# Attention and gated unit on one core: AV of the pair before and the scores of a pair side by side at the opening of a period, reciprocals ahead of the first transposes

## The chip, the core and the metric

The kernel runs on one core of a Trainium2 chip. The core has five engines that run side by side, each through its own list of instructions in order: TensorE (PE in the profile; its weight loads stand apart as PEld), VectorE (DVE), ScalarE (ACT), GpSimd (POOL) and SyncE (SP, which here only issues DMAs). TensorE writes its results into PSUM, a small memory of eight banks per partition, from which VectorE or ScalarE must take them before a bank can be used again. The metric is the device time of one execution in microseconds (us), lower is better. Time before: median 1212.31 us of three runs (1208.61 to 1212.54).

## The reference

Eight batches of eight heads of attention over 576 positions with head size 64 and a mask by blocks of 64, then a gated unit with weights 512 x 1536 twice and 1536 x 512:

```python
scores = (1 / sqrt(64)) * q @ k.T                      # 8 x 8 heads, 576 x 576
scores = where(block_i >= block_j, scores, -1e9)       # blocks of 64 positions
attn = exp(scores - max(scores)); attn /= sum(attn) + 1e-9
x = (attn @ v) -> (4608, 512)
out = (sigmoid(x @ w_gate) * (x @ w_val)) @ w_out
```

## The kernel before, in words

**Stages.** The attention and the first third of the gated unit (`F1` = 4 of 12 column blocks of the weights) run interleaved in a first stage, about 600 us. The other eight column blocks follow in a second stage, in which TensorE multiplies by a Strassen scheme (line 834). Between them lies a handover, in which VectorE prepares weights and sums for the second stage (`early_work`, lines 758 to 769, `sums_gv`, `x_sums`).

**Pairs and periods.** Two heads make a pair, four pairs a batch: 32 pairs. The loop at line 771 has a period for each pair `p`, and one more for the last AV. `attend(p)` gives the steps of a pair:

- "s", the scores (`s_blocks`, line 378): three double PSUM banks, for the query blocks 3, 2 and (1, 0). The two heads use 64 rows of the array each (`tile_position=(64 * h, 0)`, tiles of 64x128 in the profile). Then, for each group, a mask on VectorE (line 392 or 394), the negative maximum (line 372, VectorE) and two exponentials (line 375, ScalarE) into `P3`, `P2`, `P1`, `P0`, with the row sums in `sm`.
- "t", the tail of 64 queries for both heads (`s_tail`, line 398), with its maximum (408) and exponential (410).
- "r", the reciprocals (`recip`, line 413): three small VectorE instructions on `sm`, the last of which writes `rT`, then four DMAs to `r_d` in HBM and three back into `rb`, spread over the partitions; all seven are issued by SP.
- "tr3", "tr2", "trl", "trt": transposes on TensorE (line 250) of the exponentials, each into a double bank, copied by ScalarE into `G1` and `G0` (line 350, `copy_out`), of which there is one each.
- "AV" (line 472): `G1`, `G0` times `VS` (the values), the two heads in 64 columns of the array each (tiles of 128x64), 28 matmul instructions; VectorE multiplies the result by `rb` into `xT` (line 486). `finish` (491) casts `xT` to `XH` on ScalarE, stores it to HBM as `xT_d`, and GpSimd makes the low half `XL`.
- "k" and "q": steps of `prep(p + 1)`: VectorE transposes the next pair's k and q (279), ScalarE makes their high halves (314, 315), VectorE the low halves (318, 319); the loads of pair `p + 3` are issued by SP.

AV in period `p` belongs to pair `p - 1`; all other steps of the list `REST` belong to pair `p`. Double banks come from `ps_a`, of which there are three; the gated unit's products use two single banks of their own (`ps_m`).

**Order.** The order of the steps is written out in three lists: `FIRST` for pairs 0 to 6, `TURN` for pair 7, `REST` from pair 8 on (line 32). The number beside a step is its places: after the step, that many times, some instructions of the gated unit (`mlp1`: `hidden`, line 126, and `out_mm`, line 135) are dealt, `rate` of them each (lines 795 to 809). A period has `TICKS` = 12 places. `rate` is set anew when AV of a batch's last pair has been issued (lines 780 to 784), so that by the same point four periods later all but `KEEP` = 32 instructions are dealt. On TensorE the scores and AV stand behind the matmul dealt last (lines 386, 482), transposes and dealt matmuls stand behind the last scores or AV (`hold`), and a dealt matmul may be taken up to `AHEAD` = 3 places early; within that a scheduler sets each engine's order when the program is built.

**Handover.** In the last pair's period and behind it, `early_work` loads the first weights (`raw`, into tiles that held k and q of pairs 30 and 31) and the first activations (`XB` from `xT_d`), issued by SP in order, and lets VectorE make their sums.

Of the kernel before, what the change touches and what calls it, by code (L numbers as in the profile page):

```python
# [28 lines left out]

FIRST = (("s3", 1), ("TR2", 1), ("k", 1), ("s2", 1), ("TRt", 1), ("q", 1), ("t", 1), ("TRl", 1), ("sl", 1), ("AV", 2),  # L30
         ("tr3", 1), ("r", 0), ("ld", 0))
REST = (("s", 3), ("t", 1), ("AV", 2), ("tr3", 1), ("r", 0), ("k", 0), ("tr2", 1), ("q", 0), ("trl", 2), ("trt", 2))
TURN = (("s3", 1), ("TR2", 1), ("k", 0), ("s2", 1), ("TRt", 1), ("q", 0), ("t", 1), ("TRl", 1), ("sl", 1), ("AV", 1),
        ("tr3", 1), ("r", 0), ("tr2", 1), ("trl", 1), ("trt", 1))
N_FIRST = 7
# [5 lines left out]
def attn_glu_kernel(ctx: ExitStack, tc: tile.TileContext, q, k, v, w_gate, w_val, w_out, out):  # L41
# [119 lines left out]
    with ExitStack() as s2:  # L161
# [609 lines left out]
        for p in range(n + 1):  # L771
# [3 lines left out]
            tick = 0  # L775
            for what, places in (FIRST if p < N_FIRST else TURN if p == N_FIRST else REST):
                if what.startswith(("AV", "TR")):
# [247 lines left out]
```

## Time and profile before

| | |
|---|---|
| median of three runs | 1212.31 us (1208.61 to 1212.54) |
| the profiled execution's own time | 1211.92 us |
| its span, first to last instruction | 1210.1 us |
| TensorE busy | 1167.7 us (96%), 7421 matmuls |
| VectorE busy | 770.4 us (64%) |
| ScalarE busy | 627.7 us (52%) |
| GpSimd busy | 332.6 us (27%) |
| periods of the pairs from 8 on | about 16.8 us, up to 22 us where the dealt matmuls are the longer ones of line 135 |

A row of the timeline has the start, the duration, the engine, the line of the kernel, the operation, what is written from what, and the shape; equal neighbours are merged (x28), and in brackets stands how long the engine had been idle and who released it. Durations of matmuls overlap, since they are pipelined: what an instruction costs in a stream is the distance between starts. A row of busy time by stretches has the stretch, its length, then for PE, PEld, DVE, ACT and POOL the busy time and the number of instructions, then the granted clock of TensorE, the DMA share and GB/s. A row of waits has who waited, for whom, the sum in us, how many times, and the longest. The chain of waits is the work that ended last, in order of time.

### The profile page before, as it was taken

What the parts mean: (1) busy time and instruction counts of PE and PEld (TensorE: products, weight loads), DVE (VectorE), ACT (ScalarE), POOL (GpSimd) and SP (SyncE); (2) the same over time, 40 slices, a digit from 0 to 9 for tenths busy, and PEclk for the clock granted to TensorE, in tenths of its full rate; (3) what the DMA queues carried; (4) which work ended last, traced back from release to release, by engine and by line L of the source; (5) the groups of instructions that cost most, each with busy time, mean ns of one, the idle gap of its engine ahead of it and who ended that gap; (6) DMA issues with size and microseconds to landing.
All of it is one profiled execution on the core that took longest, in us unless ns stands there. A gap on an engine that the chain in (4) does not pass through costs nothing.

```text
span 1210.1 us, 20754 instructions
## 1 busy us (share of the span) xinstructions
PE 1167.7 (96%) x7421; PEld 1025.6 (85%) x7421; DVE 770.4 (64%) x1447; ACT 627.7 (52%) x1459; POOL 332.6 (27%) x411
## 2 busy tenths in 40 slices
PE   6989899999999999999999999999999999999996
PEld 3557789888888988888789889999999999998895
DVE  5678945356454545544899976866866655755743
ACT  6776857576676666666444453453454432422420
POOL 0123223133231331322101223123122153262331
PEclk8999999999999999999999999999999999999998
DMA  8664343543544443444243335235287154164153
GB/s 179 168 150 98 97 114 74 118 87 78 118 88 105 99 102 83 98 111 120 91 129 115 106 135 200 72 129 200 59 300 288 59 179 165 55 198 155 55 157 105
DMA packets 249112, 152.52 MB, mean 126 GB/s; under 512 B 189489, under 2 KB 209969, under 8 KB 248369
## 3 DMA queue, kind: packets, MB, share of 16 engines
q1 hardware_dynamic: 237952, 132.02, 39.5%
q10 hardware_dynamic: 11056, 19.17, 4.5%
q8 instruction: 58, 0.95, 0.3%
q14 instruction: 46, 0.37, 0.1%
HBM read 103.81 MB, written 47.33 MB: 125 GB/s over the span
## 4 chain that ended last, share of the span: by engine, by line
PE 73%; DVE 12%; DMA 6%; ACT 3%; POOL 2%; issue 2%; SPq 1%; POOLq 0%; DVEq 0%; ACTq 0%
PE b L834 19%; PE m L126 13%; PE bank L247 13%; PE m L892 9%; PE m L135 6%; PE bank L250 5%; PE b L892 5%; DMA pr<-part_d 3%; DVE XL L724 2%; POOL pr L907 1%; ACT P L375 1%; DMA XB<-xT_d 1%; DVE nm L372 1%; PE m L250 1%; PE bank L126 1%
## 5 line engine op out<-in xcount | busy, mean ns | idle before, releaser
L834 PE MATMUL b<-XH,w 128*128 128x384 f32 x1344 | 352.3, 337 | 5.0 <-DVE v L870 2.5
L834 PEld LDWEIGHTS b<-XH,w 128*128 128x128 f32 x1344 | 244.9, 188 | 12.4 <-DVE v L870 5.3
L834 PE MATMUL b<-XL,w 128*128 128x384 f32 x672 | 225.2, 336 | 0.0
L375 ACT ACTIVATE P<-bank,nm 128x512 f32<-128x512 f32 (+3 forms) x256 | 133.5, 538 | 69.7 <-DVE nm L372 59.0
L834 PEld LDWEIGHTS b<-XL,w 128*128 128x128 f32 x672 | 126.6, 188 | 1.3
L892 PE MATMUL m<-wo,hH 128*128 128x512 f32 x384 | 124.9, 391 | 0.0
L372 DVE TENSOR_REDUCE nm<-bank 128x2 f32<-128x1024 f32 (+3 forms) x128 | 105.0, 820 | 29.4 <-ACT P L375 26.8
L350 ACT COPY G<-bank 128x768 f32<-128x768 f32 (+3 forms) x140 | 93.2, 696 | 29.6 <-PE bank L250 26.2
L126 PE MATMUL m<-XH,wv 128*128 128x288 f32 x448 | 104.2, 304 | 1.7 <-DVE h L147 1.7
L126 PE MATMUL m<-XH,wg 128*128 128x288 f32 x448 | 104.2, 303 | 0.0
L247 PE MATMUL bank<-G,VS 128*64 128x320 f32 (+4 forms) x896 | 98.2, 361 | 0.0
L153 POOL TENSOR_TENSOR hL<-h,hH 128x288 fp32r<-128x288 f32 (+1 forms) x56 | 42.4, 757 | 199.6 <-ACT hH L152 190.7
L907 POOL TENSOR_TENSOR pr<-pr,pr 128x512 f32<-128x512 f32 x36 | 48.0, 1333 | 162.1 <-DMA pr<-part_d 139.5
L247 PEld LDWEIGHTS bank<-G,VS 128*64 128x64 f32 x896 | 55.9, 137 | 36.9 <-issue 3.5
L723 ACT CAST XH<-XB 128x1536 fp32r<-128x1536 f32 (+2 forms) x72 | 66.1, 938 | 34.6 <-DVE XB L721 25.1
L892 PEld LDWEIGHTS m<-wo,hH 128*128 128x128 f32 x384 | 71.9, 188 | 13.7
L857 ACT ACTIVATE g<-g 128x384 f32<-128x384 f32 x72 | 37.4, 524 | 81.6 <-DVE g L870 61.1
L724 DVE TENSOR_TENSOR XL<-XB,XH 128x1536 fp32r<-128x1536 f32 (+2 forms) x72 | 77.8, 1089 | 0.9 <-ACT XH L723 0.4
L126 PEld LDWEIGHTS m<-XH,wv 128*128 128x128 f32 x448 | 74.7, 188 | 4.0 <-DVE h L147 1.9
L392 DVE MEMSET bank<- 64x128 f32 x64 | 10.6, 165 | 105.8 <-PE bank L247 105.2
L126 PEld LDWEIGHTS m<-XH,wg 128*128 128x128 f32 x448 | 74.9, 188 | 3.2 <-issue 1.8
L250 PE MATMUL bank<-ident,P 128*128 128x128 f32 x560 | 75.4, 273 | 0.8 <-DVE rT L419 0.7
(179 smaller groups left out, 2488.4 us busy)
## 6 DMA issues: line engine op xcount, KB each, us to landing
pr<-part_d SPq DMA_DIRECT2D x72, 256.0 KB
xT_d<-xT ACTq DMA_DIRECT2D x32, 288.0 KB
XB<-xT_d SPq DMA_DIRECT2D x16, 576.0 KB
part_d<-ost SPq DMA_DIRECT2D x36, 256.0 KB
out_dram<-ost SPq DMA_DIRECT2D x36, 256.0 KB
VS<-in_v_dram SPq DMA_DIRECT2D x64, 128.0 KB
part_d<-ost ACTq DMA_DIRECT2D x32, 256.0 KB
rqk<-in_k_dram SPq DMA_DIRECT2D x108, 72.0 KB
```

The lines of the kernel that those rows point to most:

```text
L126: mm = nc.tensor.matmul(ps, lhsT=lh, rhs=rh, start=(i == 0), stop=(i == n - 1))
L135: mm = nc.tensor.matmul(ps, lhsT=lh[:, f, t * P:(t + 1) * P], rhs=rh, start=(i == 0), stop=(i == n - 1))
L247: pe_last[:] = [nc.tensor.matmul(*args, **kw).ins]
L250: pe_last[:] = [nc.tensor.transpose(*args).ins]
L350: mark("ACT", nc.scalar.copy(out=dst, in_=src))
L372: mark("DVE", nc.vector.tensor_reduce(out=nm[:, c0:c0 + 2], in_=ps[:, :, c:c + n], axis=AX.X, op=ALU.max, negate=True))
L375: mark("ACT", nc.scalar.activation(out=Pi[:, h], in_=ps[:, h, c:c + n], func=AF.Exp, bias=nm[:, c0 + h:c0 + h + 1], accum_out=sm[:, 5 * h ...
L723: nc.scalar.copy(out=XO[j][0][:, a:b], in_=x)
L724: sub = nc.vector.tensor_sub(out=XO[j][1][:, a:b], in0=x, in1=XO[j][0][:, a:b].bitcast(F32))
L834: mm = nc.tensor.matmul(ps, lhsT=lh, rhs=rh, start=(first and k == 0), stop=(k == n - 1), skip_group_check=not first)
L892: mm = nc.tensor.matmul(po[t], lhsT=lh[:, f, t * P:(t + 1) * P], rhs=rh, start=(half == 0 and i == 0), stop=(half == 1 and i == 5))
L907: nc.gpsimd.tensor_add(out=pr[0], in0=pr[0], in1=pr[1])
```

## The change

One list is changed. In `REST`, AV (of pair `p - 1`) moves from behind the tail to the head of the period, with no place behind it, so that the scores of pair `p` follow it on TensorE without dealt matmuls between them. Its two places go to the scores (4 instead of 3) and to "trt" (3 instead of 2). "r" moves from behind "tr3" to ahead of it. The sum of places stays 12.

```diff
-REST = (("s", 3), ("t", 1), ("AV", 2), ("tr3", 1), ("r", 0), ("k", 0), ("tr2", 1), ("q", 0), ("trl", 2), ("trt", 2))
+REST = (("AV", 0), ("s", 4), ("t", 1), ("r", 0), ("tr3", 1), ("k", 0), ("tr2", 1), ("q", 0), ("trl", 2), ("trt", 3))
```

## The prediction

> **What bounds the kernel now.** I read the page first, then the waits of TensorE over the pairs that the change touches (195 to 600 us), then busy time by stretches, single instructions around one period, and the chain of waits.
>
> ```profile
> span 1210.1 us, 20754 instructions
> PE 1167.7 (96%) x7421; PEld 1025.6 (85%) x7421; DVE 770.4 (64%) x1447; ACT 627.7 (52%) x1459; POOL 332.6 (27%) x411
> PE 73%; DVE 12%; DMA 6%; ACT 3%; POOL 2%; issue 2%; SPq 1%; POOLq 0%; DVEq 0%; ACTq 0%
> ```
> ```profile
> PE m L126 <- DVE h L147: 1.7, 1, 1.7
> PE bank L250 <- DVE rT L419: 0.7, 1, 0.7
> ```
> ```profile
> 255.30:272.10 16.80, 16.80 (x144) 15.11 (x143) 9.57 (x20) 11.67 (x32) 5.35 (x9) 1.00 0.43 91
> ```
>
> TensorE bounds it. In 405 us it waits for another engine twice, 2.4 us in all, both at the very end (below). A whole period is busy (16.80 of 16.80) at granted clock 1.00, VectorE at 9.57, ScalarE at 11.67. So nothing can be gained here by feeding TensorE sooner: only by making its own stream shorter. What is short of peak in that stream shows at the edges of the tiled blocks, where starts lie further apart than inside (one period, opening at 401.70):
>
> ```profile
> 401.47 0.29 PE L126 MATMUL m<-XL,wv 128*128 128x288 f32 x1
> 401.70 0.50 PE L247 MATMUL bank<-KH,QH 64*128 64x512 f32 x2
> 402.03 0.41 PE L247 MATMUL bank<-KH,QL 64*128 64x512 f32 x2
> 402.27 0.41 PE L247 MATMUL bank<-KL,QH 64*128 64x512 f32 x2
> ...
> 403.71 0.53 PE L126 MATMUL m<-XH,wv 128*128 128x288 f32 x2
> 404.08 0.29 PE L126 MATMUL m<-XL,wv 128*128 128x288 f32 x1
> ...
> 407.17 0.29 PE L126 MATMUL m<-XH,wv 128*128 128x288 f32 x1
> 407.40 2.93 PE L247 MATMUL bank<-G,VS 128*64 128x320 f32 x28
> 410.25 0.40 PE L126 MATMUL m<-XL,wv 128*128 128x288 f32 x1
> 410.50 0.42 PE L126 MATMUL m<-XH,wv 128*128 128x288 f32 x2
> ...
> 418.48 0.49 PE L247 MATMUL bank<-KH,QH 64*128 64x512 f32 x2
> ```
>
> The gated-unit matmuls (L126) follow each other by 0.133 us at full stream (two take 0.42 where one takes 0.29; the second decimal is rounded). Into the scores: 401.47 to 401.70 is 0.23, 0.10 too long, and the first step inside is 0.33 where the next is 0.24, 0.09 too long: 0.19 for entering. Out of them: two steps of L126 take 0.37 (403.71 to 404.08) instead of 0.27, 0.10, and I take the 0.10 before it to be as at the entry: 0.20. Into AV: 0.23 instead of 0.13, 0.10 (a little more inside it is the same after the change). Out of AV: 0.25 instead of 0.13, 0.12, with its 0.10 before: about 0.20. A period enters and leaves two tiled blocks, four edges.
>
> **The change, part by part.** (1) AV at 0 places and the scores behind it. AV's exit (0.20) and the scores' entry (0.19) go; one edge between a block of 128x64 and one of 64x128 comes. The trace has no such edge. Below: it costs nothing, and the period gains 0.39; above: it costs like the two that went, and the gain is nil; I see no way to a loss in the stream itself. I take 0.20, since the edges seen from both sides cost 0.19 to 0.22, whichever form they lead to: 0.19 gained. Pairs 8 to 31 are 24 periods: 24 x 0.19 = 4.6 us (0 to 9.4).
>
> [...]
>
> (2) What AV's earlier place demands. Before, scores, four places and the tail stood between the last transposes of a pair and its AV; now three places of about five L126 matmuls do (15 x 0.133 = 2.0 us).
>
> ```profile
> 404.36 0.69 ACT L375 ACTIVATE P<-bank,nm 128x512 f32<-128x512 f32 x1 [2.80 <-DVE nm L372]
> 409.64 0.25 ACT L375 ACTIVATION_READ_ACCUMULATOR P<-bank,nm 128x1 f32 x1
> 411.31 0.68 ACT L314 CAST KH<-KQ 128x576 fp32r<-128x576 f32 x1 [1.41 <-DVE KQ L279]
> 417.25 0.75 ACT L350 COPY G<-bank 128x512 f32<-128x512 f32 x2 [0.87 <-PE bank L250]
> ```
> ```profile
> 411.86 0.78 DVE L486 TENSOR_TENSOR xT<-bank,rb 128x320 f32<-128x320 f32 x2
> ```
> ```profile
> 410.63 1.38 SPq L422 DMA_DIRECT2D r_d<-rT  x4
> 413.77 1.74 SPq L425 DMA_DIRECT2D rb<-r_d  x3
> ```
>
> Write S for the start of the scores. The period is 16.78 (401.70 to 418.48) and AV takes 2.85 (407.40 to 410.25), so the next AV is due at S+13.9. Its last input is the copy of the tail's transposes, 0.75 us for two, which waits for TensorE, not for ScalarE (0.87 idle before it): 2.0 us cover 0.75 and 1.2 are left. Cost nothing while ScalarE keeps up (a rival, below).
>
> (3) AV's bank is wanted again by the scores' third group (three double banks turn). VectorE frees it with two products, 0.78 us, about 0.1 after AV; the first two groups stand between: 0.33 and twice 0.24 for the first, three times an estimated 0.18 for the second, three quarters as wide, 1.3 us together. Covered by 0.4.
>
> (4) The fourth product operand, rb. Its DMAs are issued until 415.51, S+13.8. It takes 1.8 us from the end of the first four issues (412.01) to the release of the next three (413.77), a round trip; the same again puts rb at about S+15.6. It was used a period later; now at S+16.9. Covered by 1.3. The reciprocals' new place ahead of tr3 moves three small VectorE instructions and these seven issues past nothing that runs earlier: they wait for the last exponential, which ends at 409.89 (S+8.2) in either order, and on SP they stand behind nothing new. I cost it at nothing; if rb slips behind the loads of q on SP, the product waits on VectorE with the mask and the maxima of the next softmax queued behind it, and TensorE waits at the third group.
>
> (5) Transposes. tr3 now stands after scores (2.0), 20 matmuls (2.7), the tail (0.8) and 5 more (0.7): S+6.2; its exponentials, 0.69 each from S+2.66, are done. tr2 comes at S+7.8, and wants the bank of the third scores group, which ScalarE leaves at S+8.2: 0.4 short. The schedule may put matmuls of the next three ticks ahead (AHEAD), so I take nothing, at most 0.4 in those periods that deal L126 matmuls alone at 5 or so a tick (three in each of five batches, 15 of 24): 6 us.
>
> (6) The dealing. Same twelve places, but the new batch opens four places earlier, so by pair 31's scores 36 instead of 32 ticks of 5.0 have passed since pair 28's AV: 20 matmuls (2.7 us) more are done; before the last AV it is 4 of L126 and 16 of L135 more (0.133 and 0.23 each, 4.2 us). That work leaves the stage behind.
>
> **Where the gain meets the handover.** The chain of waits through the last pair, then VectorE's rows, then stretches behind it:
>
> ```profile
> 564.92 2.04 PE bank L247 x20
> 568.45 7.42 DMA XB<-xT_d
> 577.70 0.68 DVE xT L486 x2
> 582.69 0.46 DVE h L147
> ```
> ```profile
> 589.22 0.39 PE L135 MATMUL m<-wo,hH 128*128 128x512 f32 x1
> 589.44 0.39 PE L135 MATMUL m<-wo,hL 128*128 128x512 f32 x1
> ```
> ```profile
> 575.96 0.56 DVE L710 TENSOR_TENSOR XB<-XB 128x384 f32<-128x384 f32 x1 [4.25 <-DMA XB<-xT_d]
> 585.21 0.29 DVE L672 TENSOR_TENSOR cT<-cT 128x128 f32<-128x128 f32 x1
> 588.69 0.82 DVE L486 TENSOR_TENSOR xT<-bank,rb 128x320 f32<-128x320 f32 x2 [3.19 <-PE bank L247]
> ```
> ```profile
> 604.00:608.00 4.00, 4.00 (x31) 3.96 (x30) 4.00 (x10) 1.34 (x3) 0.00 (x0) 1.00 0.20 68
> 608.00:612.00 4.00, 4.00 (x32) 4.00 (x31) 4.00 (x14) 1.61 (x5) 0.00 (x0) 1.00 0.44 142
> ```
>
> Here the chain is not TensorE's. Pair 31's scores free a tile, SP goes on, XB lands 7.4 us later, VectorE has stood 4.25 us for it, works, stands 3.19 us for the last AV, and from 588.69 it is full (4.00 of 4.00). So the handover ends as early as VectorE's two idle stretches allow. Pair 31's scores move by +2.85 (AV now before them) +2.7 (more matmuls before) -23 x 0.19 = -4.4: 1.2 us later. XB with them: 577.2. VectorE's work from there to the end of the row at 585.21 was 9.5 us; 0.7 of it (the product of pair 30) is now done earlier: ready at 586.0. The last AV releases the product at 588.69; minus 4.6, plus 4.2 of work dealt before it, minus the 2.4 of waits if both vanish, gives 585.9 at best, when VectorE is not yet free. If the h product is queued behind the weight sums as it is now (582.69), the L135 matmuls dealt ahead of AV wait for it, and AV about keeps its place (eight L126 matmuls and AV's 2.85 follow that product now, some seven of L135 would then): 588.3 as an estimate. So the product comes at 586.0 to 588.3: 0.4 to 2.7 us are carried to the end, I take 1.6. The other 3.0 turn into idle time of TensorE in front of a full VectorE.
>
> **Sum.** The profiled execution took 1211.92 us (span 1210.1), 0.39 under the median 1212.31 of the three. 1211.92 - 1.6 = 1210.3; against the median 1210.7. Likeliest case's own range: 1209.6 to 1211.9. A measurement of this kernel tells about 0.3%, 3.6 us, from no change.
>
> **The rivals.** A: the handover carries it all. For it: the two TensorE waits stem from VectorE standing for XB, and the pair-30 product that stands in their way moves forward. Against: rows above, XB's landing hangs on scores that move later. 1212.3 - 4.6 = 1207.7, with the 2.4 of waits 1205.3.
>
> B: slower. ScalarE becomes the bound of a period: during AV and scores, 4.9 us on end, it gets no new work but one cast, and then has the softmax and all copies before the next AV. First exponential at S+2.66; 11.67 busy less 0.68 for the cast is 11.0: done at S+13.65 if it never waits, AV due at S+13.9. If the 1.41 us it waits for KQ stays unfilled, AV is 1.1 late, in 15 periods of L126 alone 17 us: 1212.3 - 1.6 + 17 = 1228. It decides from 0.35 us a period (5.3 us less 1.6 is 3.7). Against: tr3's copy can fill that wait, and the gated unit's share of the 11.0 falls partly outside. [...]
>
> C: no net gain, as tr2's 0.4 us (part 5) eats it: -4.6 + 6, and with the handover about 1212.3 to 1214. Or the schedule puts scores ahead of AV or splits them, so that four edges stay: 1212.
>
> **How the numbers follow.** Likeliest 0.45, A 0.25, C 0.10, B 0.20. Faster by over 0.3% is A: 0.25; same is the likeliest and C: 0.55; slower is B: 0.20. The range goes from A's lower part, 1205.5, to 1218, which takes in B up to 0.6 us a period.
>
> **What would show it.** Right: between pairs 8 and 31 a period without L135 work is 16.6 instead of 16.78; AV to scores shows a first start 0.2 after AV's last; no TensorE wait before AV; pair 31's scores near 566; VectorE still full from about 587. Wrong: TensorE waits named after ScalarE's G or P at AV or tr2, each period (B, C); VectorE starting its full stretch by 584 (A).

## The result and the profile after

The changed kernel takes 1224.84 us (median of 6 runs, 1222.60 to 1226.56) against 1210.17 us (6 runs, 1207.52 to 1212.54) of the kernel before on the same chip: ratio 1.012, 95% interval 1.0101 to 1.0138. It is slower by 14.7 us, where 1210.7 with a range up to 1218 was forecast.

The page after (span, TensorE's busy time, shares of the chain that ended last):

```profile
span 1222.8 us, 20667 instructions
PE 1173.9 (96%) x7421; PEld 1027.3 (84%) x7421; DVE 780.1 (64%) x1447; ACT 624.4 (51%) x1459; POOL 322.5 (26%) x411
PE 73%; DVE 11%; DMA 6%; ACT 3%; issue 3%; POOL 2%; SPq 1%; POOLq 0%; DVEq 0%; ACTq 0%
```

The page alone hides the loss: TensorE still has 96% and 73% of the chain. Its busy time has grown by 6.2 us for the same 7421 matmuls, so part of the loss lies inside the stream. The waits of TensorE from 125 to 600 us:

```profile
PE bank L247 <- DVE xT L486: 4.1, 4, 2.8
PE bank L247 <- ACT G L350: 1.6, 1, 1.6
PE bank L247 <- ACT P L375: 0.7, 1, 0.7
PE bank L247 <- issue: 0.2, 1, 0.2
```

6.6 us, and 4.4 of them in one place, pair 8's opening. (The kernel before waits in that period too, 2.2 us for P and G, so the waits explain little by themselves.) Three places show where the rest is.

**A usual opening (pair 22).** TensorE after:

```profile
410.50 1.84 PE L247 MATMUL bank<-G,VS 128*64 128x320 f32 x12
412.27 0.50 PE L247 MATMUL bank<-KH,QH 64*128 64x512 f32 x2
...
413.16 1.31 PE L247 MATMUL bank<-G,VS 128*64 128x64 f32 x16
414.40 0.44 PE L247 MATMUL bank<-KH,QH 64*128 64x384 f32 x2
...
415.63 0.39 PE L247 MATMUL bank<-KH,QH 64*128 64x256 f32 x2 [0.44 <-DVE xT L486]
...
416.41 0.40 PE L126 MATMUL m<-XL,wv 128*128 128x288 f32 x1
```

AV isn't one block. The first group of scores stands between its first 12 and its last 16 instructions, so the two blocks meet at three edges inside instead of one, and AV ends later. The instruction order has this in 13 of the 24 openings (pairs 8, 14 to 18, 22 to 26, 30 and 31). VectorE's rows there show what follows:

```profile
413.53 1.22 DVE L372 TENSOR_REDUCE nm<-bank 128x2 f32<-128x1024 f32 x1
414.68 0.81 DVE L486 TENSOR_TENSOR xT<-bank,rb 128x320 f32<-128x320 f32 x2
```

The maxima of the first scores now stand ahead of the product that empties AV's bank; the product ends at 415.49, and the third group, which wants that bank, starts at 415.63. The same wait of 0.44 us stands at the openings of pairs 14 and 30. And ScalarE's row for the input at which AV is cut, the second tail copy:

```profile
410.51 0.28 ACT L350 COPY G<-bank 128x128 f32<-128x128 f32 x1
```

It ends at 410.79, 1.5 us before TensorE reaches the cut at 412.27. On the chip nothing had to be waited for; the cut stands in the instruction order.

**The first opening (pair 8)** on TensorE, then SP's, VectorE's rows, then stretches:

```profile
137.89 1.84 PE L247 MATMUL bank<-G,VS 128*64 128x320 f32 x12 [1.64 <-ACT G L350]
...
145.33 0.39 PE L247 MATMUL bank<-KH,QH 64*128 64x256 f32 x2 [2.75 <-DVE xT L486]
```
```profile
135.82 1.38 SPq L422 DMA_DIRECT2D r_d<-rT  x4
139.55 1.75 SPq L425 DMA_DIRECT2D rb<-r_d  x3
```
```profile
143.78 0.67 DVE L111 SCALAR_TENSOR_TENSOR XB<-csq,XB 128x512 f32<-128x512 f32 x1
144.38 0.81 DVE L486 TENSOR_TENSOR xT<-bank,rb 128x320 f32<-128x320 f32 x2
```
```profile
142.00:146.00 4.00, 1.25 (x16) 0.94 (x14) 3.97 (x9) 2.01 (x5) 0.00 (x0) 1.00 0.42 108
146.00:149.50 3.50, 3.50 (x18) 3.40 (x15) 3.44 (x5) 2.10 (x6) 1.41 (x1) 0.51 0.25 91
```

AV of pair 7 stands at once behind pair 7's last transposes, since `TURN` ends in one place where `REST` now ends in three. TensorE waits 1.64 us for their copies. rb is still on its way (its issues end at 141.30; the transfer lands at 143.66), VectorE takes one conversion more (143.78) before the product, and TensorE stands 2.75 us for the bank. Behind that the granted clock is 0.51 for 3.4 us, which costs an estimated 1.7 (half of 3.4).

**The second stage** has one long wait that the kernel before had not. SP, GpSimd, ScalarE, VectorE and TensorE in turn, each one step later, then the stretches:

```profile
721.20 3.81 SPq L906 DMA_DIRECT2D pr<-part_d  x2
725.06 1.93 SPq L902 DMA_DIRECT2D part_d<-ost  x2
```
```profile
723.37 1.29 POOL L907 TENSOR_TENSOR pr<-pr,pr 128x512 f32<-128x512 f32 x1 [11.45 <-DMA pr<-part_d]
724.62 1.01 POOL L842 TENSOR_TENSOR hL<-t,hH 128x384 fp32r<-128x384 f32 x1
```
```profile
725.66 0.49 ACT L857 ACTIVATE t<-b 128x384 f32<-128x384 f32 x1 [3.27 <-POOL hL L842]
730.53 1.55 ACT L723 CAST XH<-XB 128x768 fp32r<-128x768 f32 x2
```
```profile
731.38 1.83 DVE L724 TENSOR_TENSOR XL<-XB,XH 128x768 fp32r<-128x768 f32 x2 [2.16 <-ACT XH L723]
733.12 0.55 DVE L870 TENSOR_TENSOR v<-b,v 128x384 f32<-128x384 f32 x1
```
```profile
733.73 0.69 PE L834 MATMUL b<-XH,w 128*128 128x384 f32 x1 [3.09 <-DVE v L870]
```
```profile
729.00:733.00 4.00, 1.64 (x10) 1.32 (x8) 1.84 (x3) 4.00 (x8) 0.00 (x0) 1.00 0.43 131
733.00:736.50 3.50, 2.77 (x8) 2.68 (x9) 3.50 (x8) 2.77 (x3) 0.00 (x0) 0.52 0.00 0
```

GpSimd waits 11.45 us for a load of pr that the second half of this stage needs (SP holds it in line between two stores of ost); hL behind it, t on ScalarE, the casts XH, XL on VectorE and v all come late, TensorE stands 3.09 us, and the clock is halved once more (0.52 from 733.0 to 736.5 us).

### The profile page after: what moved, and what is told of

Same layout as the page of the kernel before. It is cut to its first block, busy times and chain, and to the rows that moved or that the text cites. A ratio compares the mean times of both kernels' runs of the same rounds, so it can differ in the third digit from the quotient of the medians.

```text
span 1222.8 us, 20667 instructions
## 1 busy us (share of the span) xinstructions
PE 1173.9 (96%) x7421; PEld 1027.3 (84%) x7421; DVE 780.1 (64%) x1447; ACT 624.4 (51%) x1459; POOL 322.5 (26%) x411
## 4 chain that ended last, share of the span: by engine, by line
PE 73%; DVE 11%; DMA 6%; ACT 3%; issue 3%; POOL 2%; SPq 1%; POOLq 0%; DVEq 0%; ACTq 0%
PE b L834 20%; PE m L126 13%; PE bank L247 13%; PE m L892 9%; PE m L135 6%; PE bank L250 5%; PE b L892 5%; DMA pr<-part_d 2%; DVE XL L724 2%; ACT P L375 1%; PE m L250 1%; POOL pr L907 1%; DMA out_dram<-ost 1%; DMA rb<-r_d 1%; DVE ost L908 1%
## 5 line engine op out<-in xcount | busy, mean ns | idle before, releaser
L834 PE MATMUL b<-XH,w 128*128 128x384 f32 x1344 | 352.4, 337 | 9.3 <-DVE v L870 3.7
L834 PEld LDWEIGHTS b<-XH,w 128*128 128x128 f32 x1344 | 245.0, 189 | 16.4 <-DVE v L870 6.7
L834 PE MATMUL b<-XL,w 128*128 128x384 f32 x672 | 225.5, 336 | 0.0
L834 PEld LDWEIGHTS b<-XL,w 128*128 128x128 f32 x672 | 126.7, 189 | 1.2
L126 PE MATMUL m<-XH,wv 128*128 128x288 f32 x448 | 104.5, 305 | 0.0
L126 PE MATMUL m<-XH,wg 128*128 128x288 f32 x448 | 104.1, 303 | 0.0
L486 DVE TENSOR_TENSOR xT<-bank,rb 128x320 f32<-128x320 f32 x64 | 26.3, 452 | 120.0 <-PE bank L247 95.9
L247 PE MATMUL bank<-G,VS 128*64 128x320 f32 (+4 forms) x896 | 101.1, 363 | 1.6 <-ACT G L350 1.6
L496 POOL TENSOR_TENSOR XL<-xT,XH 128x576 fp32r<-128x576 f32 x32 | 46.4, 1451 | 182.6 <-ACT XH L493 171.4
L126 PEld LDWEIGHTS m<-XH,wv 128*128 128x128 f32 x448 | 76.0, 190 | 1.4 <-issue 0.5
L126 PEld LDWEIGHTS m<-XH,wg 128*128 128x128 f32 x448 | 75.5, 189 | 1.9 <-issue 0.9
L892 PE MATMUL m<-wo,hL 128*128 128x512 f32 x192 | 75.6, 394 | 0.0
```

The costliest lines, as they stand in the source:

```text
L126: mm = nc.tensor.matmul(ps, lhsT=lh, rhs=rh, start=(i == 0), stop=(i == n - 1))
L247: pe_last[:] = [nc.tensor.matmul(*args, **kw).ins]
L834: mm = nc.tensor.matmul(ps, lhsT=lh, rhs=rh, start=(first and k == 0), stop=(k == n - 1), skip_group_check=not first)
L892: mm = nc.tensor.matmul(po[t], lhsT=lh[:, f, t * P:(t + 1) * P], rhs=rh, start=(half == 0 and i == 0), stop=(half == 1 and i == 5))
```

## The experiments

Each ratio is to runs of the kernel before on the same chip: 1208.35 us beside experiments 1 to 4, 1209.33 beside 5 to 7, 1208.84 beside 8 to 10 and 1208.71 beside 11 and 12. Added lines shift the numbers in their rows by up to four. Where the trace is read at fixed points, these are the start of pair 9's scores, of pair 31's scores, of the first product of the second stage (L834 in the kernel before) and of TensorE's last matmul. In the kernel before they are at 157.8, 564.8, 641.5 and 1199.7 us, after at 168.0, 578.5, 650.0 and 1212.3. Kernels 5 and 12 have the same first stage, and their first products lie 2.8 us apart (641.8 and 639.0), so differences of 1 or 2 us at that point say little by themselves. A trace is one execution: those of 5, 8 and 10 took 5.1, 2.4 and 3.0 us more than the median of their runs, so sums of costs below go by the medians.

**1. Scores behind the whole AV, in all pairs.**

```diff
+                        if av_last and k == j == 0:
+                            behind(first_mm[0], av_last[0])
...
+                av_last[:] = pe_last
```

> The changed kernel with one order added: the scores of a pair stand behind the last matmul of AV on TensorE, so that AV cannot be split. Theory (the split is the scheduler's choice; on the chip the copies that AV needs were done long before): all 24 openings become one AV and one scores block; the 13 split ones lose 0.56 to 1.04 us each (the first, of pair 8, keeps its wait for rb), 9.8 us in all: 1214 to 1217 us. Rival (ScalarE is really late for AV): TensorE then waits inside AV for the G copies, 0.5 us or more in some ten periods, and the time stays at 1221 or above.

1224.92 us, ratio 1.0139 (1.0122 to 1.0155). All 24 openings are whole, and from pair 9's scores to pair 31's it is 404.1 us instead of 410.5 after and 407.0 before. But the hold also acted on pairs 0 to 7, whose lists were not meant: pair 9's scores start at 176.6 instead of 168.0. So this total, above the 1214 to 1217 expected, tells nothing about the splits; experiment 5 repeats it from pair 8 on alone.

**2. The list of before in the period of pair 8 alone.**

```diff
+REST8 = (("s", 3), ("t", 1), ("AV", 2), ("tr3", 1), ("r", 0), ("k", 0), ("tr2", 1), ("q", 0), ("trl", 2), ("trt", 2))
...
-            for what, places in (FIRST if p < N_FIRST else TURN if p == N_FIRST else REST):
+            for what, places in (FIRST if p < N_FIRST else TURN if p == N_FIRST else REST8 if p == N_FIRST + 1 else REST):
```

> The changed kernel with the old list in the period of pair 8 alone, the new list from pair 9. Theory: the 1.6 us for a G copy, the 2.8 us for the product that waits for rb, and the slower TensorE clock behind them (13 matmuls at 0.24 instead of 0.13 us, 1.4 us) go, about 6 us; splits stay in about ten of the 23 remaining openings (in others than before): 1215 to 1219 us. Rival (the waits of pair 8 are absorbed later anyway): 1222 to 1226.

1211.49 us, ratio 1.003 (1.002 to 1.0041). One period out of 24 gives back 11.6 of the 14.7 us, more than expected, although ten openings are still split.

**3. Both edits, 1 and 2.**

> Both: scores held behind AV, and the old list for pair 8. Theory (nothing else costs): 23 openings save 0.19 us each, 4.4 us, of which the handover lets 0.4 to 4.4 us through: 1206 to 1210, or 0.2 to 4.4 us below the kernel before. Rival (the new place of AV costs something on its own, as tr2 waiting for its bank): above the kernel before by 2 us or more, with TensorE waits in each period.

1215.29 us, ratio 1.006 (1.0044 to 1.0076). Missed, for the reason of experiment 1: pair 9's scores start at 171.2 although pair 8 has its old list.

**4. "r" back behind "tr3".** Otherwise as changed.

```diff
-REST = (("AV", 0), ("s", 4), ("t", 1), ("r", 0), ("tr3", 1), ("k", 0), ("tr2", 1), ("q", 0), ("trl", 2), ("trt", 3))
+REST = (("AV", 0), ("s", 4), ("t", 1), ("tr3", 1), ("r", 0), ("k", 0), ("tr2", 1), ("q", 0), ("trl", 2), ("trt", 3))
```

> The changed kernel with the reciprocals back behind the first transposes. Theory (they wait for the last exponential in either place, so their place in the list decides nothing): the same as the changed kernel, 1222 to 1227. Rival (their earlier place helps or hurts by 2 us or more through SP's queue): a difference of over 3 us.

1226.79 us, ratio 1.015 (1.0131 to 1.0169): the intervals of this and of the change overlap. The order on every engine is the same in both, instruction by instruction. The move of the reciprocals is worth nothing, as forecast. (Its second stage takes 564.5 us by the trace, the change's 562.3: so much can lie between two executions of one order.)

**5. Scores behind the whole AV, from pair 8 on** (edit 1 with `if rest and av_last and ...`).

> The changed kernel, with the scores held behind the last matmul of AV on TensorE only from pair 8 on (the earlier hold also acted on pairs 0 to 7, where it cost time of its own). So all 24 openings are unsplit and pairs 0 to 7 are as in the changed kernel. Theory (two causes: splits in 13 openings, and the opening of pair 8, where TensorE waits for the copies to G and for rb): pair 9's scores still start near 168.0 us, since in pair 8 the wait for rb ends at the same instant whether AV is split or not; from there to pair 31's scores 404.1 us instead of 410.5, as in the earlier hold; of these 6.4 us nearly all reach the end, because VectorE's handover hangs on pair 31's scores and the last AV: 1216 to 1219, still slower than before. Rival 1 (the splits are the whole loss): 1209 or less. Rival 2 (the handover takes what the splits give back, the splits cost nothing): 1223 to 1226, with the first product of the second stage near 650 as in the changed kernel.

1212.73 us, ratio 1.0031 (1.0013 to 1.0048). Pair 9's scores start at 168.0 and pair 31's 403.6 later, both as the theory had them, but the total falls by some 11 us instead of 6 to 9. The same opening of pair 22, TensorE and VectorE:

```profile
406.93 2.93 PE L247 MATMUL bank<-G,VS 128*64 128x320 f32 x28
409.79 0.50 PE L247 MATMUL bank<-KH,QH 64*128 64x512 f32 x2
...
410.95 0.34 PE L247 MATMUL bank<-KL,QH 64*128 64x384 f32 x2
411.23 0.39 PE L247 MATMUL bank<-KH,QH 64*128 64x256 f32 x2
...
412.00 0.40 PE L126 MATMUL m<-XL,wv 128*128 128x288 f32 x1
```
```profile
410.25 0.82 DVE L489 TENSOR_TENSOR xT<-bank,rb 128x320 f32<-128x320 f32 x2 [3.34 <-DMA rb<-r_d]
```

The two blocks take 5.07 us (406.93 to 412.00) instead of 5.91 (410.50 to 416.41): a split costs 0.84 here, and thirteen at that price would be an estimated 10.9 us, about what the total fell by. The product still waits for rb, but only 0.1 us of it reaches TensorE (411.23 for 411.13).

**6. Edits 5 and 2 together.**

> Both remedies: the list of before for the period of pair 8 alone, and scores behind the whole AV from pair 8 on, with pairs 0 to 7 left as they are. Theory: pair 9's scores near 158.8 us (as with the old list for pair 8), then 406.3 us to pair 31's scores and 474 us to the first product of the second stage (as with the earlier hold and the old list, which had both remedies but a disturbed start), then the second stage as before: 1203 to 1208, faster than before by 0.2 to 0.6%. Rival (a cost of the new order beyond splits and pair 8, about 3 us by the first run with both remedies): 1209 to 1213. Rival (the handover takes it back): first product of the second stage near 641 as with the old list for pair 8 alone, 1210 to 1212.

1210.14 us, ratio 1.0009 (0.9999 to 1.002): missed, no gain. The trace splits it in two. The first product of the second stage comes at 637.1, 4.4 us earlier than before; from there to the last matmul it takes 562.6 us instead of 558.2, so all of it is lost again in the second stage, where TensorE waits 3.5 us for v and the clock is halved behind that, as shown above for the change (matmuls of 128x384 start 0.32 us apart at 721.5, 0.18 apart at 730.2).

**7. The new list for pair 8 alone**, the list of before from pair 9 on.

> The new list in the period of pair 8 alone, the list of before from pair 9 on: one split opening instead of 13, so the price of pair 8's opening by itself. Theory: pair 9's scores about 7.3 us later than before (10.2 in the changed kernel, less 2.86 for an AV that stands ahead of them there), 165.1 us; the rest keeps its lengths, so 1216 to 1219 without further loss, and up to 1221 if the later loss in the second stage (two stretches of half clock there instead of one) belongs to pair 8's delay. Rival (pair 8's opening is harmless by itself and the loss comes from the order of later pairs): 1209 to 1213.

1212.98 us, ratio 1.0034 (1.0022 to 1.0047). TensorE stands 1.66 us for G and 2.76 for the product as in the change, and pair 9's scores start at 163.8, near the 165.1 expected. By itself this opening costs 3.6 us: the waits at pair 8 are 2.2 us longer than before (4.4 for 2.2), and a stretch of half clock behind them (from 145.4 to 148.5 us matmuls of 128x288 start 0.24 us apart, at 149.0 0.13) costs an estimated 1.7. The total lies where the rival expected it, but above before by more than the interval.

**8 to 10. pr's loads held back in the second stage**: on both remedies (8), on the kernel before (9), on the change (10).

```diff
-                        nc.sync.dma_start(out=part2_d[r:r + P, :], in_=ost)
+                        stored[:] = [nc.sync.dma_start(out=part2_d[r:r + P, :], in_=ost).ins]
...
-                        mark2("SP", nc.sync.dma_start(out=tile_, in_=src[r:r + P, :]))
+                        d = nc.sync.dma_start(out=tile_, in_=src[r:r + P, :])
+                        behind(d.ins, stored[0])
+                        mark2("SP", d)
```

> Both remedies as in the run before (list of before in pair 8's period alone, scores behind the whole AV from pair 8 on), and in the second stage the loads of pr (L906) held on SP behind the last store of the first round of blocks, so that they no longer stand between the stores of ost. In both remedies alone the first product of the second stage came 4.4 us earlier than before (637.1 against 641.5), and the second stage gave 4.3 us back: from its first product to TensorE's last 562.5 us against 558.2, with one wait of 3.5 us for VectorE at 717 to 721 and a stretch of half clock behind it. Theory (the scheduler's other order in the second stage costs this, by the loads of pr on SP and what stands behind them): the wait goes, second stage 556 to 559 us, total 1203 to 1206, faster than before by 0.3 to 0.5%. Rival (the second stage is bound by VectorE's work from the handover on, so that an earlier start only turns into waits): first product near 637, second stage still 562, total 1209 to 1211.

> Control: the kernel before with the same hold on the loads of pr alone. Its second stage has no such wait (2.0 us for VectorE's g once), so theory: within 1 us of before, 1208 to 1210, second stage 557 to 559. If it is faster than before by as much as the kernel with both remedies is, the gain there is the hold's and not the new order's.

> The changed kernel with the same hold on the loads of pr alone. Its second stage took 562.3 us against 558.2 of before, with a wait of 3.1 us for VectorE's v and half clock from 733. Theory (three causes: pair 8's opening, the splits, the second stage's order): the first product of the second stage stays near 650, the second stage falls to 557 to 559, total 1219 to 1222. Rival (the second stage's loss follows from a late handover, whatever its order): total 1223 to 1226.

8: 1207.28 us, ratio 0.9985 (0.9973 to 0.9997). 9: 1208.44, ratio 0.9999 (0.9988 to 1.001). 10: 1219.95, ratio 1.0088 (1.0072 to 1.0104). The hold is worth nothing on the kernel before and 3.6 us on the change (14.7 to 11.1). 9 and 10 came as expected; 8 lies between the 1203 to 1206 of its theory and the 1209 to 1211 of its rival. In 8, TensorE's wait shrinks but stays:

```profile
PE b L838 <- DVE g L874: 2.6, 1, 2.6
PE b L838 <- DVE v L874: 2.4, 3, 1.8
```

The longest wait for v is 1.8 instead of 3.5, the stage 560.0 us instead of 562.6. So the order of pr's loads is one part. The rival, that a full VectorE turns an earlier start into waits, is not shown for the rest: VectorE is as full in kernel 11 (below) as in 6, whose first products come at 636.3 and 637.1, and the second stage of 11 takes 557.1 us. Kernel 6, then 11:

```profile
640.00:665.00 25.00, 23.92 (x137) 23.39 (x137) 25.00 (x49) 11.38 (x21) 4.76 (x4) 1.00 0.25 80
```
```profile
640.00:665.00 25.00, 23.93 (x136) 23.14 (x135) 25.00 (x49) 11.27 (x20) 4.75 (x4) 1.00 0.20 60
```

**11 and 12. What AV of pair 7 lacks.** 12 is the change with edit 5 and the hold on pr; 11 is that with three of pair 8's places moved ahead of AV ("ld" does nothing in this period).

```diff
+REST8 = (("ld", 3), ("AV", 0), ("s", 3), ("t", 1), ("r", 0), ("tr3", 1), ("k", 0), ("tr2", 1), ("q", 0), ("trl", 1), ("trt", 2))
```

> The changed kernel with scores behind the whole AV from pair 8 on and the loads of pr held back in the second stage, the new list from pair 8 on: what is left of the loss is pair 8's opening alone. Theory: pair 9's scores near 168.0 us with the waits of 1.6 us for G and about 2.8 us for the product (rb) at pair 8 and a stretch of half clock behind them; total as the kernel with both remedies and the same hold (1207.3) plus the 2.6 us that pair 8 cost between the two kernels that have the unsplit order (1212.7 against 1210.1): 1209 to 1212.

> The same kernel, with three of pair 8's twelve places moved ahead of AV of pair 7 (one each from the scores, trl and trt), so that some ten matmuls more stand on TensorE between pair 7's last transposes and that AV. Theory (AV of pair 7 comes too early for the copies to G and for rb, since pair 7's own list leaves one place or none behind its last transposes): the wait for G of 1.6 us goes, the wait for the product shrinks from 2.8 to about 1.5 us, too short for the stretch of half clock; pair 9's scores fall from 168.0 to 162.5 to 164 us; the total falls by 1 to 3 us against the kernel without it, to 1207 to 1210. Rival (the loss at pair 8 lies in the scores' and transposes' order there, not in AV's inputs): pair 9's scores stay at 167 or later and the total does not fall.

12: 1209.17 us, ratio 1.0006 (0.9989 to 1.0023). 11: 1206.26, ratio 0.9984 (0.9972 to 0.9997). In the trace of 11 at pair 8:

```profile
138.46 2.93 PE L248 MATMUL bank<-G,VS 128*64 128x320 f32 x28 [1.66 <-ACT G L351]
...
144.79 0.38 PE L248 MATMUL bank<-KH,QH 64*128 64x256 f32 x2 [1.97 <-DVE xT L490]
```

The numbers came in, the mechanism mostly not. The wait for G stays (the dealt matmuls spread between the transposes, which moved with AV), and the wait for the product falls to 1.97, from 2.60 in 12, with the half clock behind it all the same (0.50 from 145.9 to 149.3 us). That 1.5 us would be too short for it was the author's estimate; behind the changed kernel's wait of 1.64 us the clock is 1.00 (138 to 142 us). Pair 9's scores start at 163.6 instead of 167.2, but ten matmuls of L135 fewer lie ahead of them, some 2.3 us that are merely done later. 11 is faster than 12 by 2.9 us; in the traces its first product of the second stage comes 2.7 us earlier (636.3 for 639.0), and that stage takes 557.1 us instead of 558.7, in an order on TensorE and VectorE that no other kernel here has. So the gain is not shown to be AV's later place.

## Why the prediction was wrong, point by point

The start of AV's last product on VectorE, then the starts of TensorE, us, and the totals against before. "Order" names the second stage's order of instructions on TensorE and VectorE, which is the same in every kernel with the same letter:

| kernel | list at pair 8 | AV | AV's last product | first product, 2nd stage | from it to the last matmul | order | total, us |
|---|---|---|---|---|---|---|---|
| before | old | apart | 588.7 | 641.5 | 558.2 | a | 0 |
| 9 (before, pr held) | old | apart | 587.6 | 640.2 | 558.7 | a | -0.4 |
| 7 | new | split at 8, then apart | 591.0 | 645.1 | 556.6 | a | +3.6 |
| 6 | old | whole | 588.9 | 637.1 | 562.6 | b | +0.8 |
| 5 | new | whole | 592.9 | 641.8 | 563.0 | b | +3.4 |
| changed | new | split | 600.6 | 650.0 | 562.3 | b | +14.7 |
| 8 (6 with pr held) | old | whole | 589.1 | 637.2 | 560.0 | b | -1.6 |
| 12 (5 with pr held) | new | whole | 590.1 | 639.0 | 558.7 | b | +0.5 |
| 10 (changed, pr held) | new | split | 602.1 | 651.5 | 558.8 | b | +11.1 |
| 2 | old | split | 593.0 | 641.1 | 558.2 | its own | +3.1 |
| 11 | new, AV later | whole | 588.3 | 636.3 | 557.1 | its own | -2.4 |

**The step that failed** is a premise of part 1 and of the likeliest case, taken without a reason: that the schedule would keep AV whole and that 24 periods are alike, pair 8's included. Rival C named the split, but as no dearer than the four edges of before. What the runs showed in its place, by the totals: the splits cost 11.3 us (5 to the change), the new list at pair 8 costs 2.6 (6 to 5), and with neither the kernel is 0.8 slower than before: 14.7 together. With the loads of pr held it is 10.6 (12 to 10), 2.0 (8 to 12) and -1.6.

Kernel 6 is the nearest to what was predicted, with 23 new openings instead of 24. Its first product of the second stage comes 4.4 us earlier, where part 1 had 4.6, but that is luck: AV's last product, through which the forecast carried the gain, starts 0.2 us later than before. The 4.4 come from the handover behind it, 48.2 us instead of 52.8; it takes 48.0 to 49.5 in the table's kernels of order b or of an order of their own, and 52.7 to 54.1 in those of order a. Nothing in the prediction had that.

The second stage was not in the prediction either. In order b (kernels 1 and 4 have it too) it takes 562.3 to 564.5 us, whether it starts at 637 or at 650, and 558.7 to 560.0 with the loads of pr held; in order a 556.6 to 558.7, held or not. So these 4 us belong to the order, with pr's loads as the main part of it, and not to a late or an early start.

(1) The edge was about right. Pair 21's scores before, then in kernel 5:

```profile
384.94 0.50 PE L247 MATMUL bank<-KH,QH 64*128 64x512 f32 x2
```
```profile
393.24 0.51 PE L247 MATMUL bank<-KH,QH 64*128 64x512 f32 x2
```

Pair 22's follow at 401.70 and 409.79: the period takes 16.55 us against 16.76, with 60 dealt matmuls in both, 0.21 gained for 0.19 forecast. Not every period gains it. The next one takes 17.00 in kernel 5 and 16.75 in kernel 12, against 16.78 before; in both kernels, dealt matmuls stand between the last of its transposes. Over the 22 periods from pair 9's scores to pair 31's, kernels 5 and 12 are 3.4 and 3.7 us shorter than before (403.6 and 403.4 for 407.0), about 0.16 a period; their 20 dealt matmuls of L126 more and 12 of L135 fewer cancel.

(2) AV's last input was in time on the chip in the usual openings, as worked out, and this did not help: the instruction order is fixed when the program is built, and there AV is cut at the piece that takes the second tail copy. That the scheduler reckons this copy later than the chip has it is argued from where the cut stands, not shown. What the hold shows is that nothing on the chip forced it: with AV whole, behind pair 8 TensorE waits for the copies at AV 0.19 and 0.16 us in kernel 5 and not at all in 12.

(3) AV's bank: nearly covered where AV is whole and rb is there in time (0.1 us at pair 22 of kernel 5), not where AV is split, since VectorE then takes the maxima first: 0.44 at pair 22.

(4) rb was mis-sized. The prediction put it at S+15.6, by a round trip of 1.8 us; in kernel 5 the product at pair 22's opening, AV of pair 21, is released by rb at 410.25, 17.0 us after that pair's scores at 393.24. The cover of 1.3 us is none: three of the products at its 24 openings waited for rb in the end, and in kernel 8 such a wait at pair 23 holds TensorE for 1.45 us. At pair 8, whose AV has no places before it, the lack is 2.75 us of TensorE. "Covered" had been worked out for a period between two new lists, not for the one behind `TURN`. The reciprocals' move was free (experiment 4).

(5) The bank of tr2: no such wait in the trace, 0 as taken.

(6) The dealing and the handover: pair 31's scores were put at 566.0 and start at 566.66 in kernel 6. The product of the last pair was put at 586.0 to 588.3; there:

```profile
588.89 0.82 DVE L490 TENSOR_TENSOR xT<-bank,rb 128x320 f32<-128x320 f32 x2 [3.28 <-DMA rb<-r_d]
```

AV had ended at 586.7, inside the forecast; rb came last once more, and VectorE's full stretch begins 0.2 us later than before (588.69), so of the 0.4 to 2.7 us that were to be carried to the end none is. The mis-sized term is rb again. That kernel 8, with the loads of pr held, is 1.6 us faster than before is the forecast's size by luck: its last product of AV starts at 589.11, and its gain comes behind that.

Rivals: A did not happen. B's mechanism did not either: behind pair 8 no period of the changed kernel waits for ScalarE. C named the split but priced it at the four edges of before, 1212, without the later end of AV, and without VectorE's order. The range's end, 1218, came from B; no case held that split openings could be dearer than the old order.

**What stays open.** The two losses are not additive: the new list at pair 8 costs 2.6 us where AV is whole (6 to 5) and 11.6 where it is split (2 to changed). About 4 of these 9 us are the second stage's order, since 2 has its own (558.2 us) and the other three share order b. The rest lies ahead of the second stage and was not traced. Nor was it traced which decision of the scheduler cuts AV in some openings and not in others, or gives the second stage one order or another.

The best version measured is 11, 1206.26 us, with 8 close behind: both beat the kernel before by about 0.15%, with intervals that end at 0.03%, and the change by 1.3%.

## What to carry to other kernels

When steps are moved next to each other, the order that the scheduler writes has to be read before anything is priced: an accumulation block may be cut in two where nothing on the chip forces it (13 of 24 openings here), and an explicit order between its last matmul and the next block is cheap (waits of 0.19 and 0.16 us at AV in kernel 5). Price the first period behind a change of lists by itself; there the old list's ending feeds the new list's opening. An early gain in a stream is only worth something if the work behind it can start earlier: here rb came last, so that VectorE's full stretch began no earlier (588.89 us in kernel 6, 588.69 before), and a prefetch standing ahead in two queues lengthened the second stage (562.3 us in the changed kernel, 558.8 with it held back).

## What the runs showed of the hardware that was not expected

The granted clock drops to half for 3.4 us (or twice that) at a few places. In the changed kernel it is 0.50 from 16.4 to 23.1 us, 0.51 from 146.0 to 149.5 and from 682.0 to 685.4, and 0.52 from 733.0 to 736.5. In the kernel before it is 0.50 from 15.8 to 22.5 and from 671.1 to 674.5. The stretches stand at or just behind a gap of TensorE: in the changed kernel of 2.75 us at pair 8, of 2.54 (to 681.10) and of 3.09 (to 733.73), in the kernel before of 2.02 (to 671.47), and in kernel 11 of 1.97 at pair 8. It is not the gap's length alone. In kernel 12 the same opening has a wait of 2.60 and no such stretch; there the stretch is at 87 us, behind a gap of 1.81 us:

```profile
86.92 2.23 PE L247 MATMUL bank<-KQ,QB 128*128 128x288 f32 x4 [1.81 <-ACT P L375]
```
```profile
85.00:87.00 2.00, 0.19 (x2) 0.08 (x1) 1.98 (x5) 1.58 (x5) 0.00 (x0) 1.00 0.00 1
87.00:90.40 3.40, 3.40 (x11) 2.83 (x12) 3.40 (x7) 2.66 (x8) 1.55 (x1) 0.50 0.79 146
...
143.00:146.00 3.00, 0.46 (x6) 0.14 (x2) 1.79 (x5) 0.05 (x1) 0.00 (x0) 1.00 0.59 146
146.00:150.00 4.00, 3.94 (x34) 3.85 (x35) 3.91 (x9) 2.70 (x7) 1.60 (x1) 1.00 0.20 76
```

The kernel before and the changed kernel have a gap of 1.82 us near 87 us too, and the clock behind it is 1.00 in both (87.0 to 93.0 us). So gaps of about 2 us have a stretch of half clock behind them in some of these traces and not in others. What decides it is not shown.

And rb's small transfers took longer than the round trip read from the queue: at pair 8 the last of three is issued by 141.30 and the data are usable at 143.66, 2.4 us later, after 2.2 us for the step before it (137.20 to 139.41). From the chain of the changed kernel:

```profile
136.89 2.52 DMA r_d<-rT
140.69 2.96 DMA rb<-r_d
```
